# Output chunks of the feed-forward part copied from PSUM by VectorE and ScalarE in turn, with another table of priorities

## The chip, the cores and the metric

The kernel runs on one core of one Trainium2 chip. The core has TensorE (PE in the profile), which multiplies matrices into PSUM, VectorE (DVE), ScalarE (ACT) and GpSimd (POOL) for elementwise work, and SyncE (SP), which here issues most of the DMAs. The metric is device time in microseconds; several executions are timed, and one more is taken by the hardware profiler.

## The reference

Threshold attention over 8 batches and 8 heads (576 positions, head size 64), followed by a gated feed-forward part on the 4608 resulting rows of 512:

```python
scores = scale * np.matmul(q, k.transpose(0, 1, 3, 2))
thresh = np.max(scores, axis=-1, keepdims=True) - tau
scores = np.where(scores >= thresh, scores, -1000000000.0)
attn = np.exp(scores - np.max(scores, axis=-1, keepdims=True))
attn = attn / (np.sum(attn, axis=-1, keepdims=True) + 1e-09)
x = np.matmul(attn, v)                      # heads side by side: 4608 x 512
xn = x / np.sqrt(np.mean(x * x, axis=-1, keepdims=True) + 1e-06) * rms_g
g = xn @ w_gate                             # 512 -> 1536
silu = g * (1.0 / (1.0 + np.exp(-g)))
out = (silu * (xn @ w_val)) @ w_out         # 1536 -> 512
```

## The kernel before

**Work and tiles.** The 4608 rows are cut into 36 chunks of 128 (32 of them 128 positions of one batch, kind "m", and 4 that join the last 64 positions of two batches, kind "v"). For each chunk there are four steps, one for each pair of heads: 144 steps. A step makes the scores of two heads for 128 rows into `s_ps` (PSUM, L697), copies them negated and scaled to `ssb` while it takes their minimum (VectorE, L730), adds tau on GpSimd (L771), and runs one prelu for each head and one exp for both on ScalarE (L782, L789). A DMA transpose on SyncE's queue (L849), in the first 16 steps TensorE (L834), turns the weights into `wt`; two steps together are multiplied with the values (L870, L875), divided by their sum on VectorE (L892, L893) and put into `xsb`. When a chunk's four steps are done, `emit_x` normalises it (square on ScalarE L910, two small operations and a product on GpSimd L913 to L918) and a DMA transposes it into `xnT`.

**The feed-forward part.** `emit_ffn` works on groups of chunks (SIZES: two groups of 2, then eight of 4). For each of 12 blocks of the inner dimension: four matmuls for the gate (L976) and four for the value (L981), each into one PSUM bank of `ring`; tanh on ScalarE (L990), silu on VectorE (L993), product on VectorE (L998) into `hf` (half of its buffers are the staging tile `stg`). Then each chunk of the group gets twelve matmuls with `wo` (L1047) into one bank of `ring`, in two parts of six, and an eviction `ev` copies the bank, multiplied by 0.5, into an output buffer `osb`: a `tensor_scalar` on VectorE (L1062) or an `activation` with Copy on ScalarE (L1064). `store` then writes it out from SyncE's queue (L1075, L1078, L1083). Before the last group two `osb` buffers alternate by chunk. The last group is "streamed" (STREAMED = 1): its four outputs accumulate while its blocks are still computed (L1022), two of its chunks are evicted on VectorE and two on ScalarE, the final one in two halves (L1068 is the first), and ScalarE issues some of its stores.

Which engine evicts a chunk of the other nine groups is chosen by

```python
late = streamed and j % 2
on_dve = streamed and not late or not streamed and OUT_DVE[ci % len(OUT_DVE)]
```

where `ci` is the number of the chunk. `OUT_DVE` is (1,): all 32 go to VectorE.

**What sets the order.** Every operation is added to a list with its engine, an assumed cost, its dependences and a priority in units of steps. `order_ops` then plays the kernel through with the assumed costs: for each engine it takes, of the operations that could start first, the one with the lowest priority number, and the result is written out as the fixed order of each engine's instructions. PSUM banks are handed out in the same pass: `ring` starts with four free banks (two halves of `s_ps` come to it at the end), and an eviction gives its bank back. Before that a table `RANK` shifts priorities, for operations whose priority is 8 or more and not on SyncE; the key is the function that adds the operation and the name of the inner function:

```python
if o.prio >= 8.0 and o.eng != "SP":
    path = o.fn.__qualname__.split(".")
    o.prio += RANK.get(o.eng, {}).get((path[-3] if ... else "main") + "/" + path[-1], 0.0)
```

A positive shift puts an operation behind others that are ready at the same time. The eviction has the priority of its place in the group less 40 (`PUSH[0]`), tanh the same push, silu and the product none. `main/<lambda>` on GpSimd are the four loads of `wo` (L1145), `main/cast` the casts of the other weights (L1133), `emit_block_loads/swap` copies that rearrange k and q (L390), `round_/<lambda>` the casts of v (L584), `emit_softmax/nthr` L771.

Of the kernel before, what the change touches and what calls it, by code (L numbers as in the profile page):

```python
# [12 lines left out]

LAT = dict(PE=200.0, ACT=130.0, DVE=175.0, POOL=20.0, SP=0.0)
SELF = dict(PE=0.0, ACT=125.0, DVE=178.0, POOL=0.0, SP=0.0)
COST = dict(
# [7 lines left out]
SWITCH = 125.0  # L24

RANK = dict(
    ACT={"emit_ffn/ev": 450, "emit_ffn/store": 110, "emit_ffn/tanh": -300, "emit_k_tail/ev": -210, "emit_q_tail/ev": -80, "emit_qk/ev": 370,
        "emit_softmax/ex2": 60, "emit_softmax/prelu": 220, "emit_x/sq": -330},
    DVE={"emit_blocks/turn_k": 120, "emit_blocks/turn_kt": 288, "emit_blocks/turn_q": 293, "emit_burst/ttr": -57.4, "emit_ffn/ev": 320,
        "emit_ffn/gate": 60, "emit_ffn/silu": -59, "emit_k_tail/ev": 80, "emit_qk/ev": -20, "emit_softmax/ev": 320, "emit_x/ev": 50},  # L30
    PE={"emit_av/fn": -370, "emit_burst/fn": 16, "emit_ffn/gmm": 20, "emit_ffn/omm": 23, "emit_ffn/vmm": -40, "emit_k_tail/tr": 210, "emit_q_tail/tr":
        -160, "emit_qk/tr": 60, "emit_softmax/tr": -40, "emit_x/trp": 20},
    POOL={"emit_block_loads/swap": 40, "emit_softmax/nthr": -240, "emit_x/mean": -150, "emit_x/norm": -10, "round_/<lambda>": 130, "main/<lambda>":
        700, "main/cast": -280},
)


# [18 lines left out]
def order_ops(ops, ring_sizes):  # L56
# [26 lines left out]
    while len(out) < len(ops):  # L83
        best = None
        for e, lst in pending.items():
# [5 lines left out]
            for i in lst:  # L91
                o = ops[i]
                t = max(t0, ready_at[i])
                if o.ring is not None:
# [3 lines left out]
                    t = max(t, sorted(free)[o.nring - 1][0])  # L98
                other = e == "PE" and o.mode != mode
                t = max(t, o.release)  # L100
# [11 lines left out]
        cost = o.cost  # L112
        if e == "PE":
            if o.mode != mode:
# [35 lines left out]
def kernel(  # L150
# [98 lines left out]
    def gated(o, step):  # L249
        gates.append((o, step))  # L250
        return o

    def add(eng, cost, prio, deps, fn, **kw):
        o = Op(eng, cost, prio, deps, fn, **kw)
        ops.append(o)
        return o
# [30 lines left out]
    def setup():  # L287
        o_id = add("POOL", 2000.0, -100, [], lambda o: make_identity(nc, id32))

        def zero(o):  # L290
            nc.vector.memset(zcol, 0.0)
            nc.vector.memset(xn[0], 0.0)

        o_z = add("DVE", 350.0, -200, [], zero)

        def warm(o):

            for _ in range(WARM):
                nc.tensor.matmul(s_ps[0][:, 0:512], xn[0][:, 0:128], xn[0], start=True, stop=True)

        o_w = add("PE", WARM * 380.0, -200, [o_z], warm)

        def consts(o):
            nc.vector.tensor_copy(out=id16, in_=id32)
            nc.vector.memset(mhalf, -0.5)

        def vconst(o):
            for i in range(2):
                nc.vector.memset(va[i][:, :, :, D:D + 1], 1.0)
                nc.vector.memset(va[i][64:128, :, 8], 0.0)  # L310
                nc.vector.memset(va[i][0:64, :, 9], 0.0)

        o_c = add("DVE", 300.0, -100, [o_id, o_z], consts)
        o_v = add("DVE", 2000.0, -90, [], vconst)
        o_g = add("SP", 350.0, -0.5, [], lambda o: nc.sync.dma_start(
            out=rmsg, in_=moe_rms_g.rearrange("(c p) -> p c", p=128)), dma=100.0)
        return o_id, o_c, o_v, o_g
# [4 lines left out]
    def emit_qk(b, p, prio):  # L322
# [13 lines left out]
        def tr(o):  # L336
            for j in (1, 0):
                for c in range(4):
                    for r, rs in enumerate(HALF):
# [4 lines left out]

        t = gated(add("PE", COST["tr_qk"], -500.0, los + [o_id] + last_s.get(("k", b - 2, p), []), tr, ring="R",
                      nring=2, mode=1), prio)
        done = []
        for r, rs in enumerate(HALF):
            def ev(o, r=r, rs=rs):
                src = ring[t.slot[r]].rearrange("p (j c n) -> p j c n", j=2, n=64)  # L350
                if EVAC[r] == "ACT":
                    nc.scalar.copy(out=dst[:, :, :, rs], in_=src)
                else:
                    nc.vector.tensor_copy(out=dst[:, :, :, rs], in_=src)

            done.append(add(EVAC[r], COST["evac_qk" if EVAC[r] == "DVE" else "evac_qk_act"], prio, [t], ev, frees=(t, r)))
        for j in range(2):
# [7 lines left out]
    def emit_block_loads(b, g, base, prio):  # L365

        done = {}
        for j, src in ((1, k), (0, q)):
# [14 lines left out]
            for h in range(2):  # L383
# [4 lines left out]
                for dst, at in moves:  # L388
                    def swap(o, dst=dst, at=at):
                        nc.gpsimd.tensor_copy(out=dst, in_=at)  # L390

                    last = [add("POOL", COST["swap"], prio + SWAP_AT, last, swap)]
                spare_use.append(last[0])
# [28 lines left out]
    def emit_first():  # L422
# [13 lines left out]
        def load_k(p, prio):  # L436
# [6 lines left out]

            return add("SP" if p else "ACT", COST["sp_qk"], prio, before, load, dma=DMA_NS["qk"], bulk=True)

# [10 lines left out]
        def transposed(load, srcs, dsts, prio, engines):  # L456
# [9 lines left out]
            for e, (eng, lo, hi) in enumerate(engines):  # L466
                def ev(o, eng=eng, lo=lo, hi=hi):
                    copy = nc.scalar.copy if eng == "ACT" else nc.vector.tensor_copy
                    for i, m, dst in dsts:
                        if lo <= i < hi:  # L470
                            rs = slice(dst.base_partition(), dst.base_partition() + dst.shape[0])
                            copy(out=dst, in_=ring[t.slot[0]][rs, n * i:n * (i + m)].rearrange("p (a n) -> p a n", n=n))
# [13 lines left out]
        def emit_k(p, load, prio):  # L486
            nat = qkn[p % NQK]
            t, k_ready[p] = transposed(load, [pair(nat[:, 1, c]) for c in range(4)],
                                       [(0, 2, qkT[0][p][:, 0, 0:2]), (2, 2, qkT[0][p][:, 0, 2:4])], prio,
                                       [("ACT" if p in (1, 2) else "DVE", 0, 2), ("ACT", 2, 4)])  # L490
            tr_of[1].append(t)
# [84 lines left out]
    def emit_v(b, prio):  # L576
# [6 lines left out]
        def round_(dst, src):  # L583
            return lambda o: nc.gpsimd.tensor_scalar(out=dst, in0=src, scalar1=1.0, scalar2=1.0,  # L584
                                                     op0=ALU.mult, op1=ALU.mult)

        def free(p):
            return [o_v] + last_av.get((b - 2, p), [])

        for p in range(NP):  # L590
# [12 lines left out]
            if b >= BLOCKED and p == 0:  # L603
                lo = []
                for i in range(2 * V_PARTS):
# [8 lines left out]
                    lo[-1].lat = LAT_V  # L614
            ca = add("POOL", COST["cast_v"], (pr + V_CAST if b >= BLOCKED else pr + 1 if b else p - 1.0), (lo[2 * (p * V_PARTS // NP):][:2] if b >= BLOCKED else lo) + free(p), round_(
                t[:, p, 0:8, 0:D].rearrange("q (c h) d -> q h c d", h=2),
# [3 lines left out]
            if p == 0:  # L620
# [6 lines left out]
                for e in range(2):  # L627
                    es = slice(64 * e, 64 * e + 64)
                    ca = add("POOL", COST["cast_vt"], (pr + 1.3 if b else -0.5), [lt] + [x for p in range(NP) for x in free(p)],
                             round_(t[es, :, 8 + e, 0:D], vtl[es]))  # L630
# [322 lines left out]
    def emit_ffn(slot, parts, ready_step, pace, streamed):  # L953
# [81 lines left out]
        for j, (ci, _) in enumerate(parts):  # L1035
# [19 lines left out]
            late = streamed and j % 2  # L1055
            on_dve = streamed and not late or not streamed and OUT_DVE[ci % len(OUT_DVE)]

# [130 lines left out]
TTR_E = 0.0  # L1188
TTR_TO = 16
SQ_DVE = (0,)  # L1190
OUT_DVE = (1,)
LAGS = ()
CHOP = ((32, 144),)
TTR_PRIO = 0.0
# [92 lines left out]
```

## Time and profile before

| | us |
|---|---|
| median of 4 runs | 534.71 |
| lowest and highest of them | 533.09 and 536.46 |
| profiled execution, its own time | 535.12 |
| span of its trace | 533.3 |
| TensorE busy | 521.5 |
| VectorE busy | 465.7 |
| ScalarE busy | 443.9 |
| GpSimd busy | 224.0 |

The trace gives every instruction with its start and duration. In the groups, "out<-in" names the tiles written and read, "x" counts instructions, then come busy microseconds, the mean nanoseconds of one, and the idle time of the engine before them with what ended it. In tables by stage each row is a stretch of the span; the columns are TensorE, its weight load, VectorE, ScalarE and GpSimd with busy microseconds and instruction counts, then the granted clock of TensorE (1.00 is full), the share of the DMA engines in use and GB/s. Ends of matmuls are modelled, so their starts are the safer reading. The first score matmul runs at 6.6 us, the first feed-forward matmul at 62.4, the first output matmul at 89.2, and the first eviction at 93.4.

### The profile page before, as it was taken

What the parts mean: (1) busy time and instruction counts of PE and PEld (TensorE: products, weight loads), DVE (VectorE), ACT (ScalarE), POOL (GpSimd) and SP (SyncE); (2) the same over time, 40 slices, a digit from 0 to 9 for tenths busy, and PEclk for the clock granted to TensorE, in tenths of its full rate; (3) what the DMA queues carried; (4) which work ended last, traced back from release to release, by engine and by line L of the source; (5) the groups of instructions that cost most, each with busy time, mean ns of one, the idle gap of its engine ahead of it and who ended that gap; (6) DMA issues with size and microseconds to landing.
All of it is one profiled execution on the core that took longest, in us unless ns stands there. A gap on an engine that the chain in (4) does not pass through costs nothing.

```text
span 533.3 us, 14401 instructions
## 1 busy us (share of the span) xinstructions
PE 521.5 (98%) x5368; PEld 275.1 (52%) x5368; DVE 465.7 (87%) x1348; ACT 443.9 (83%) x648; POOL 224.0 (42%) x478
## 2 busy tenths in 40 slices
PE   8899999999999999999999999999999999999996
PEld 4566776654545454545454544454544454454442
DVE  4799999979999799989997999999999898865741
ACT  5999999989997899889987898989998999962210
POOL 2278667425762155717733265626652111111000
PEclk9999999999999999999999999999999999999999
DMA  9999989979978888999889798998898678653013
GB/s 186 233 291 299 231 141 190 190 123 242 194 157 170 158 172 182 152 202 207 172 171 176 146 178 172 201 216 166 171 191 139 118 118 134 128 111 70 14 27 98
DMA packets 218886, 88.51 MB, mean 166 GB/s; under 512 B 195264, under 2 KB 204992, under 8 KB 218816
## 3 DMA queue, kind: packets, MB, share of 16 engines
q1 hardware_dynamic: 216016, 85.49, 81.1%
q0 software_dynamic: 1600, 1.57, 1.9%
q8 instruction: 42, 0.69, 0.6%
q10 hardware_dynamic: 1200, 0.52, 0.5%
q14 instruction: 28, 0.23, 0.1%
HBM read 37.75 MB, written 9.44 MB: 88 GB/s over the span
## 4 chain that ended last, share of the span: by engine, by line
PE 63%; DVE 16%; ACT 6%; DMA 5%; issue 4%; POOL 3%; SPq 1%; DVEq 0%; POOLq 0%; ACTq 0%
PE s_ps L697 19%; PE ring L1047 12%; PE ring L981 11%; PE ring L976 11%; DVE ssb L730 10%; PE ring L875 4%; ACT ssb L782 3%; PE s_ps L1022 2%; DVE sl L993 2%; DMA wt<-wsb 2%; DMA qkx<-in_q_dram 2%; DVE hf L998 1%; PE ring L870 1%; ACT wsb L789 1%; PE s_ps L1047 1%
## 5 line engine op out<-in xcount | busy, mean ns | idle before, releaser
L782 ACT ACTIVATE ssb<-ssb,nth 128x576 f32<-128x576 f32 x288 | 209.2, 766 | 21.4 <-POOL nth L771 20.8
L730 DVE CUSTOM_DVE_ANT_0 ssb<-s_ps,zcol 128x576 f32<-128x576 f32 (+8 forms) x288 | 169.4, 635 | 6.5 <-PE s_ps L697 4.9
L697 PE MATMUL s_ps<-qkt 64*64 64x288 f32 (+8 forms) x2256 | 170.4, 412 | 0.8 <-DVE mx L730 0.8
L789 ACT ACTIVATE wsb<-ssb 128x1152 f16<-128x1152 f32 x144 | 166.7, 1158 | 2.6 <-DMA wt<-wsb 0.5
L697 PEld LDWEIGHTS s_ps<-qkt 64*64 64x64 f32 x2256 | 82.1, 134 | 65.4 <-issue 29.0
L976 PE MATMUL ring<-xnT,wg 128*128 128x512 f16 (+1 forms) x464 | 109.2, 358 | 0.6 <-DVE sl L993 0.5
L981 PE MATMUL ring<-xnT,wv 128*128 128x512 f16 (+1 forms) x456 | 107.0, 357 | 0.5 <-DVE sl L993 0.2
L990 ACT ACTIVATE th<-ring 128x512 f32<-128x512 f32 (+1 forms) x116 | 62.5, 541 | 39.4 <-PE ring L976 39.1
L771 POOL TENSOR_SCALAR nth<-mx 128x2 f32<-128x2 f32 x144 | 30.8, 214 | 150.1 <-DVE mx L730 141.2
L993 DVE SCALAR_TENSOR_TENSOR sl<-th,ring 128x512 f32<-128x512 f32 (+1 forms) x116 | 72.0, 623 | 11.3 <-ACT th L990 11.1
L981 PEld LDWEIGHTS <-wv 128*128 128x128 f16 x480 | 44.5, 98 | 50.3 <-issue 11.1
L976 PEld LDWEIGHTS <-wg 128*128 128x128 f16 x480 | 42.9, 98 | 52.6 <-issue 15.1
L730 DVE CUSTOM_DVE_ANT_0 ssb<-s_ps,zcol,mxp 128x128 f32<-128x128 f32 (+7 forms) x112 | 52.9, 509 | 13.7 <-PE s_ps L697 13.6
L875 PE MATMUL ring<-va,wt 128*128 128x65 f16 (+1 forms) x1280 | 51.1, 193 | 0.0
L875 PEld LDWEIGHTS <-wt 128*128 128x128 f16 (+1 forms) x1280 | 46.1, 100 | 5.0 <-issue 0.6
L1047 PE MATMUL ring<-wo,hf 128*128 128x512 f16 x204 | 47.7, 380 | 0.0
L998 DVE TENSOR_TENSOR stg<-ring,sl 128x512 f16<-128x512 f32 (+1 forms) x57 | 35.5, 627 | 2.4
L998 DVE TENSOR_TENSOR hf<-ring,sl 128x512 f16<-128x512 f32 (+1 forms) x57 | 35.5, 626 | 1.8
L1047 PE MATMUL ring<-wo,stg 128*128 128x512 f16 x156 | 36.5, 379 | 0.0
L390 POOL COPY spare<-qkx 32x576 f32<-32x576 f32 x48 | 31.6, 658 | 9.8 <-DMA qkx<-in_k_dram 4.3
L893 DVE TENSOR_TENSOR xsb<-ring,rz 128x256 f32<-128x256 f32 x72 | 30.5, 424 | 3.5
L1047 PEld LDWEIGHTS <-hf 128*128 128x128 f16 x216 | 20.0, 98 | 25.8 <-issue 3.5
(75 smaller groups left out, 483.1 us busy)
## 6 DMA issues: line engine op xcount, KB each, us to landing
vst<-in_v_dram SPq DMA_DIRECT2D x32, 256.0 KB, 4.3
qkx<-in_k_dram SPq DMA_DIRECT2D x24, 288.0 KB, 3.6
qkx<-in_q_dram SPq DMA_DIRECT2D x24, 288.0 KB, 3.8
out_dram<-osb SPq DMA_DIRECT2D x48, 128.0 KB, 2.7
stg<-in_moe_w_gate_dram SPq DMA_DIRECT2D x6, 512.0 KB, 6.1
stg<-in_moe_w_val_dram SPq DMA_DIRECT2D x6, 512.0 KB, 6.1
wt<-wsb SPq DMA_TRANSPOSE x128, 3.6
out_dram<-osb SPq DMA_DIRECT2D x8, 256.0 KB, 3.0
```

Of the source, the lines that this page charges most:

```text
L390: nc.gpsimd.tensor_copy(out=dst, in_=at)
L697: nc.tensor.matmul(s_ps[h][rows, at:at + hi - lo], lhs(hs), k_of(bb, p, h)[hs, lo:hi], start=True, stop=True)
L730: nc.vector.tensor_tensor_reduce(out=ssb_of(s)[:, h, lo:hi], in0=s_ps[h][:, at:at + hi - lo], in1=zcol.to_broadcast([128, hi - lo]), scale ...
L782: nc.scalar.activation(out=sb_[:, h], in_=sb_[:, h], func=PRELU, scale=-1.0, bias=nth[m][:, h:h + 1], **PRELU_KW)
L789: nc.scalar.activation(out=wsb[s % NW], in_=sb_, func=AF.Exp)
L875: nc.tensor.matmul(ring[o.slot[0]][rs, at:at + D + 1], w[:, 5 * h + j, rs], va[vi][:, p, 2 * j + h], start=False, stop=(h == 1 and j == 3))
L976: nc.tensor.matmul(ring[o.slot[0]][:, 0:n], wg[d][:, fs], xnT[slot][:, d, 0:n], start=(d == 0), stop=(d == 3))
L981: nc.tensor.matmul(ring[o.slot[0]][:, 0:n], wv[d][:, fs], xnT[slot][:, d, 0:n], start=(d == 0), stop=(d == 3))
L990: nc.scalar.activation(out=th[i][:, 0:n], in_=ring[g.slot[0]][:, 0:n], func=AF.Tanh, scale=0.5)
L993: nc.vector.scalar_tensor_tensor(out=sl[i][:, 0:n], in0=th[i][:, 0:n], scalar=1.0, in1=ring[g.slot[0]][:, 0:n], op0=ALU.add, op1=ALU.mult)
L998: nc.vector.tensor_tensor(out=hf[hi][:, 0:n], in0=ring[vv.slot[0]][:, 0:n], in1=sl[i][:, 0:n], op=ALU.mult)
L1047: nc.tensor.matmul(ring[(first or o).slot[0]], hf[hs[fc][0]][:, 128 * j:128 * (j + 1)], wo[:, fc], start=(fc == 0), stop=(fc == NFC - 1))
```

## The change

`OUT_DVE` becomes (1, 0): of the 32 chunks before the streamed group those with an even number are evicted by VectorE and those with an odd number by ScalarE. The table `RANK` is another one: some shifts have other values, some are gone (`emit_ffn/ev` on both engines, `emit_x/sq`, `emit_av/fn`, `emit_ffn/vmm`, `main/<lambda>`), and two are new (`emit_av/half`, `emit_ffn/ev_half`). Costs, sizes, buffers and the operations themselves are as they were.

```diff
 RANK = dict(
-    ACT={"emit_ffn/ev": 450, "emit_ffn/store": 110, "emit_ffn/tanh": -300, "emit_k_tail/ev": -210, "emit_q_tail/ev": -80, "emit_qk/ev": 370,
-        "emit_softmax/ex2": 60, "emit_softmax/prelu": 220, "emit_x/sq": -330},
-    DVE={"emit_blocks/turn_k": 120, "emit_blocks/turn_kt": 288, "emit_blocks/turn_q": 293, "emit_burst/ttr": -57.4, "emit_ffn/ev": 320,
-        "emit_ffn/gate": 60, "emit_ffn/silu": -59, "emit_k_tail/ev": 80, "emit_qk/ev": -20, "emit_softmax/ev": 320, "emit_x/ev": 50},
-    PE={"emit_av/fn": -370, "emit_burst/fn": 16, "emit_ffn/gmm": 20, "emit_ffn/omm": 23, "emit_ffn/vmm": -40, "emit_k_tail/tr": 210, "emit_q_tail/tr":
-        -160, "emit_qk/tr": 60, "emit_softmax/tr": -40, "emit_x/trp": 20},
-    POOL={"emit_block_loads/swap": 40, "emit_softmax/nthr": -240, "emit_x/mean": -150, "emit_x/norm": -10, "round_/<lambda>": 130, "main/<lambda>":
-        700, "main/cast": -280},
+    ACT={"emit_ffn/store": 90, "emit_ffn/tanh": -280, "emit_k_tail/ev": -180, "emit_q_tail/ev": -130, "emit_qk/ev": 440, "emit_softmax/ex2": 160,
+        "emit_softmax/prelu": 210},
+    DVE={"emit_av/half": 50, "emit_blocks/turn_k": 140, "emit_blocks/turn_kt": 256, "emit_blocks/turn_q": 260, "emit_burst/ttr": -58,
+        "emit_ffn/ev_half": -40, "emit_ffn/gate": 70, "emit_ffn/silu": -58.6, "emit_k_tail/ev": 70, "emit_qk/ev": -40, "emit_softmax/ev": 250,
+        "emit_x/ev": 60},
+    PE={"emit_burst/fn": 10, "emit_ffn/gmm": 20, "emit_ffn/omm": 23, "emit_k_tail/tr": 240, "emit_q_tail/tr": -300, "emit_qk/tr": 30,
+        "emit_softmax/tr": -2, "emit_x/trp": 10},
+    POOL={"emit_block_loads/swap": 120, "emit_softmax/nthr": -220, "emit_x/mean": -180, "emit_x/norm": 110, "round_/<lambda>": 110, "main/cast":
+        -250},
 )
...
-OUT_DVE = (1,)
+OUT_DVE = (1, 0)
```

## The prediction

> **What bounds the kernel now.** I read the page's head first (span, busy time by engine), then the table by stage, then PE's timeline in a stretch with evictions.
>
> ```profile
> span 533.3 us, 14401 instructions
> ...
> PE 521.5 (98%) x5368; PEld 275.1 (52%) x5368; DVE 465.7 (87%) x1348; ACT 443.9 (83%) x648; POOL 224.0 (42%) x478
> ...
> PE 63%; DVE 16%; ACT 6%; DMA 5%; issue 4%; POOL 3%; SPq 1%; DVEq 0%; POOLq 0%; ACTq 0%
> ```
>
> The third line is the chain that ended last: TensorE carries 63% of it, and the hops through VectorE and ScalarE are short pieces between matmuls. The stages say where the slack lies (TensorE, its weight load, VectorE, ScalarE, GpSimd, each busy us of the stretch):
>
> ```profile
> 20.00:50.00 30.00, 27.48 (x366) 19.33 (x362) 26.89 (x77) 27.47 (x41) 20.34 (x40) 1.00 1.09 285
> 50.00:100.00 50.00, 49.83 (x643) 33.63 (x641) 48.30 (x140) 49.52 (x80) 33.84 (x65) 1.00 0.97 195
> 100.00:150.00 50.00, 50.00 (x568) 26.90 (x565) 46.32 (x149) 46.44 (x69) 25.18 (x54) 1.00 0.96 183
> ...
> 200.00:250.00 50.00, 50.00 (x511) 24.95 (x510) 48.34 (x146) 45.69 (x66) 26.28 (x56) 1.00 1.02 190
> ...
> 400.00:450.00 50.00, 49.49 (x558) 24.24 (x556) 44.61 (x136) 46.26 (x67) 10.18 (x29) 1.00 0.76 127
> ...
> 480.00:500.00 20.00, 20.00 (x109) 9.28 (x106) 13.34 (x21) 5.39 (x10) 1.43 (x3) 1.00 0.21 47
> ```
>
> TensorE is full from 50 us on, at full granted clock, while VectorE and ScalarE run at 87 to 99% beside it until about 475 us; then attention is done and 50 us of feed-forward matmuls remain for which neither is needed much. A busy TensorE need not run at its best pace, so I measured the pace from its timeline:
>
> ```profile
> 215.88 1.04 PE L981 MATMUL ring<-xnT,wv 128*128 128x512 f16 x4
> 216.75 2.75 PE L1047 MATMUL ring<-wo,stg 128*128 128x512 f16 x12
> ...
> 220.03 1.96 PE L697 MATMUL s_ps<-qkt 64*64 64x256 f32 x32
> 221.92 4.06 PE L1047 MATMUL ring<-wo,stg 128*128 128x512 f16 x18
> 225.91 1.96 PE L697 MATMUL s_ps<-qkt 64*64 64x384 f32 x32
> ```
>
> Start to next start: four matmuls 0.87 us, a burst of 32 score matmuls 1.89, eighteen output matmuls 3.99 (0.22 each). I did this for all runs of matmuls of one line, and took from each the shortest time of a run with the same count and shapes and the same kind of successor (score burst or not). What is above that is TensorE's lost time: 14.7 us in all, of it 2.6 in 0 to 20, 3.3 in 20 to 50, 2.6 in 50 to 100, then by stretches of 50 us 0.82, 1.17, 0.48, 0.89, 0.63, 0.96, 1.06 (sum 6.0 from 100 to 450), and 0.2 after that. The matmuls themselves are not touched by the change, so a gain must come out of these 14.7 us, and the first evicted output chunk starts only at 93.4 us: for the evictions themselves at most about 6 us are there to be won.
>
> **The evictions (OUT_DVE).** Nine of the ten feed-forward groups, 32 chunks, are evicted on VectorE now; the last, streamed group keeps its own rule. With (1, 0) the 16 chunks with an odd index go to ScalarE. The prices:
>
> ```profile
> L1062 DVE TENSOR_SCALAR osb<-ring 128x512 f32<-128x512 f32 x30 | 20.1, 676 | 10.5 <-PE ring L1047 10.5
> ...
> L1064 ACT ACTIVATE ssb<-s_ps 128x512 f32<-128x512 f32 x1 | 0.6, 597 | 8.9 <-PE s_ps L1022 8.9
> ```
>
> and, from VectorE's timeline, two in a row:
>
> ```profile
> 225.39 1.28 DVE L1062 TENSOR_SCALAR osb<-ring 128x512 f32<-128x512 f32 x2
> ```
>
> VectorE gives back 16 x 0.676 = 10.8 us (two in a row took 1.28, so at least 16 x 0.60 = 9.6, the second start being one 0.68 before the end); ScalarE takes 16 x 0.597 = 9.6 us (less where the next follows at once: in ScalarE's timeline the 0.57 us tanh at 177.66 had its successor start at 178.13, so at least 16 x 0.47 = 7.5). Busy time becomes about 455 on VectorE and 453 on ScalarE. Stores stay on SyncE, in the same number and with the same buffer for each chunk, since chunk parity was already buffer parity.
>
> VectorE's relief: in the seven stretches from 100 to 450 us TensorE's loss does not follow VectorE's load (48.3 busy with 0.48 lost, 44.6 with 1.06), so I take 0; at best half of the 6.0 us goes, -3, and it can cost nothing.
>
> ScalarE's load: the 9.6 us spread over about 375 us, 1.3 more in each 50. Behind a waiting eviction on ScalarE stand prelu and exp of the next softmax steps (2 x 0.77 + 1.16 us a step), and behind these SyncE's transpose of the weights, the attention-value matmuls and the score buffers. Two rows bound it. Against 100 to 450 (mean 45.56 busy, 0.86 lost) the stretch 50 to 100 (49.52 busy, 2.63 lost) gives 1.77/3.96 = 0.45 us lost for one of load: +4.3. Within the seven stretches the loss does not rise with ScalarE's load (43.3 busy with 0.89, 46.4 with 0.63 to 0.96): 0. I take +1.5, nearer to the seven, which are the stage concerned.
>
> The function change on ScalarE costs nothing by the trace. The page has one table load for the whole kernel, though ScalarE changes between prelu, exp, tanh, square and copies all along:
>
> ```profile
> L472 ACT ACT_TABLE_LOAD x1 | 1.3, 1283 | 1.5 <-PEq L1268 1.5
> ```
>
> If each of the 16 copies brought two such loads, ScalarE would get 16 x 2 x 1.283 = 41 us more; the two copies at 526 and 528 us brought none, so I take 0. ("ScalarE: Activation LUTs", Table sets, asks to batch calls by set and puts a switch at some 2.7 us, which would speak against the change; 32 switches would be 86 us by it. It also says that cheap functions like copy are in every set, and that agrees with the row.) "TensorEngine Tiling (Array Packing)", PSUM Bottleneck, says to use both engines for evacuation, which by itself would make this a gain of up to VectorE's 10.8 us; the trace shows TensorE full without it, so the sum has 0 for that.
>
> **The priorities (RANK).** They reorder every engine but SyncE's own entries, for operations with a due step of 8 or more. Evictions on VectorE go from rank +320, behind everything ready, to 0 with their push of 40: ahead of all but reductions, silu and input copies. In the trace evictions started 0.04 to 5.88 us after their last matmul (216.75 + 2.75 = 219.51 against 225.39 above). A sooner eviction frees one of four banks sooner; TensorE lost 0.48 us in that very stretch, so this is worth 0 to -0.5, and I take 0. On VectorE the attention output drops to +50; on TensorE attention-value goes from -370 to 0 and the value matmul from -40 to 0; on ScalarE the square goes from -330 to 0. Work only changes places, TensorE's queue runs strictly as written, and every place in which the written order is wrong by a few tenths of a us is lost. The largest single losses after 100 us were 0.64, 0.48 and 0.35. Bounds: half of the 8.5 us lost before 100 us is recovered (-4), or one 0.3 us wait comes with each of the 16 moved chunks and the early stage loses as much again as it does from 20 to 100 (+4.8 + 5.9 = +10.7). No row of the trace favours a side, and I take 0.
>
> The loads of the output weights on GpSimd lose their +700. They go out at 41.9 to 59.7 us now, with the DMA engines at share 1.0; earlier they push 1.5 MB ahead of other loads, each 384 KB / 285 GB/s = 1.4 us. All four lie inside the full stage already, so the total there does not change: 0, bounds -1.4 and +1.4. The swaps, at rank 120 instead of 40, come later on GpSimd, which is busy 42% of the time: 0.
>
> The tail is the same: streamed group, last evictions and stores are unchanged (520 to 533 us).
>
> **Sum.** +1.5 us on the profiled execution's 535.12 us (span 533.3 and 1.8 around it) is 536.6; that execution lies 0.4 above the median of the runs, 534.71, so the forecast for the median is 536.2.
>
> **The rivals.** About 0.5%, 2.7 us, is what a measurement of this kernel can tell from no change.
>
> Slower by more than that: ScalarE becomes late. It is at 93% in the full stages and goes to about 95%; in a row of three prelus and an exp a copy in the middle, waiting for its twelfth matmul, holds back softmax, and TensorE finds neither scores nor gates ready. For: 50 to 100 us, the one stretch with ScalarE at 99%, loses three times as much as the others. Against: 475 to 525 us holds 50 us of matmuls that can be drawn forward when attention is late. It decides from 0.17 us lost for each moved chunk on (2.7/16); at 0.3 it gives 534.7 + 4.8 = 539.5, with the early stage worse too up to 545.
>
> Faster: VectorE is what ends the small waits, and with 10.8 us less on it and banks freed at once half of the 6.0 us goes, with a part of the early loss: 534.7 - 3 - 1 = 530.7. For: VectorE is the busier of the two, and it carries 16% of the chain. Against: the losses do not follow its load.
>
> That it does nothing on the chip but swap slack is the forecast itself, with TensorE full: 533 to 537.
>
> **How the numbers follow.** Forecast case (within 0.5%) 0.43, ScalarE late 0.38, VectorE's relief 0.19. The forecast's own range is 532 to 537.4; to leave out no more than 2 in 10 it reaches to 530.7 below and 542.5 above. Slower has more than faster, since 6 us can be won in the stage concerned and more can be lost.
>
> **What would show it.** VectorE near 455 and ScalarE near 453 us busy; 16 copies from line 1064 near 0.6 us on osb; still one table load; TensorE's matmul count unchanged and its lost time, counted as above, near 16 us. Score bursts or gate matmuls that wait for prelu or tanh say ScalarE is late. The prediction is wrong if the new order loses time in the first 100 us, or if it wins there what I give to no one.

## The result, and the profile after

The changed kernel takes 535.1 us (median of 51 runs, 533.79 to 538.34) against 534.28 for the kernel before beside it (74 runs); the ratio is 1.0016, 95% interval 1.0010 to 1.0022. That is 0.85 us slower, by the bound of 0.5% no change. The prediction was 536.2, in a range of 530.7 to 542.5, with "within 0.5%" as the likeliest case. The profiled execution took 534.77 us (span 533.0), 0.35 less than the one before the change, so 0.85 us cannot be looked for in the two traces.

The head of the page after: span, busy time by engine, and the chain that ended last.

```profile
span 533.0 us, 14390 instructions
...
PE 521.4 (98%) x5368; PEld 276.1 (52%) x5368; DVE 455.7 (86%) x1332; ACT 451.0 (85%) x664; POOL 224.2 (42%) x478
...
PE 85%; DVE 6%; DMA 3%; issue 2%; POOL 1%; SPq 1%; ACT 1%; DVEq 0%; POOLq 0%
```

VectorE went from 465.7 to 455.7, ScalarE from 443.9 to 451.0, TensorE stayed. The chain now has 85% TensorE instead of 63%, which looks like a great change and is worth nothing: its shares moved without any time moving. (Perhaps because, where three engines are nearly full, a chain followed back through one may as well be followed through another; no run shows it.) The groups of the evictions and the table load:

```profile
L1063 DVE TENSOR_SCALAR osb<-ring 128x512 f32<-128x512 f32 x15 | 10.2, 679 | 4.5 <-PE ring L1048 3.7 <-DMA out_dram<-osb 0.8
...
L1065 ACT ACTIVATE osb<-ring 128x512 f32<-128x512 f32 x16 | 9.4, 585 | 17.2 <-PE ring L1048 12.3 <-DMA out_dram<-osb 4.9
...
L473 ACT ACT_TABLE_LOAD x1 | 1.3, 1283 | 1.5 <-PEq L1269 1.5
```

(Lines after the table are one higher than before.) Sixteen copies on ScalarE at 585 ns, and still one table load. By stage (TensorE, its weight load, VectorE, ScalarE, GpSimd busy us, then clock, DMA share, GB/s):

```profile
50.00:100.00 50.00, 50.00 (x644) 33.58 (x637) 48.22 (x140) 48.95 (x79) 33.45 (x65) 1.00 0.92 193
100.00:150.00 50.00, 50.00 (x566) 27.52 (x569) 45.03 (x147) 47.11 (x71) 24.65 (x54) 1.00 0.93 181
...
200.00:250.00 50.00, 50.00 (x509) 25.32 (x507) 47.08 (x147) 45.45 (x67) 25.84 (x54) 1.00 0.96 185
...
400.00:450.00 50.00, 50.00 (x575) 24.94 (x574) 44.56 (x137) 48.25 (x69) 9.92 (x30) 1.00 0.81 130
```

TensorE's lost time, counted by the prediction's rule, is 14.7 us: 2.4 in 0 to 20, 3.5 in 20 to 50, 2.9 in 50 to 100, then 1.11, 1.03, 1.09, 0.93, 0.74, 0.31 and 0.47 by stretches of 50 us (5.7 from 100 to 450). For the kernel before, the prediction's 14.7 is 0.7 too small. Between two steps of attention-value matmuls at 290.3 us, 0.68 us are lost while TensorE waits for the transposed attention weights (the last bracket is the idle time and what ended it):

```profile
291.25 0.23 PE L870 MATMUL ring<-va,wt 128*128 128x130 f16 x1 [0.50 <-DMA wt<-wsb]
```

With it the kernel before loses 15.4 us, 6.7 of them from 100 to 450 us and 1.57 instead of 0.89 in 250 to 300; it is also the largest single loss after 100 us. The readings of the prediction stand with these numbers.

This count is the yardstick of all that follows. As an estimate, time moves by what is added to or taken from TensorE's work plus the change of its lost time:

| run | lost time, us | ratio to the kernel before, 95% interval |
|---|---|---|
| before | 15.4 | 1 |
| changed kernel | 14.7 | 1.0016 (1.0010 to 1.0022) |
| engines alone | 15.2 | 1.0000 (0.9990 to 1.0010) |
| table alone | 16.6 | 1.0007 (0.9993 to 1.0022) |
| evictions twice, VectorE | 24.0 | 1.0166 (1.0151 to 1.0181) |
| evictions twice, ScalarE | 16.6 | 1.0043 (1.0029 to 1.0058) |
| fewer matmuls | 20.8 | 0.9863 (0.9839 to 0.9887) |
| half copies | 15.8 | 1.0009 (0.9993 to 1.0024) |
| more on VectorE, elsewhere | 31.0 | 1.0298 (1.0266 to 1.0330) |
| more on ScalarE | 24.3 | 1.0188 (1.0164 to 1.0212) |
| all on ScalarE | 19.8 | 1.0085 (1.0055 to 1.0114) |
| tiny copies | 14.5 | 1.0025 (1.0005 to 1.0045) |
| fewer matmuls, tiny copies | 19.0 | 0.9829 (0.9800 to 0.9857) |
| all but one on ScalarE | 15.0 | 1.0011 (0.9998 to 1.0024) |

(In the run with all on ScalarE the score burst ahead of its longest wait is written as 16 matmuls of 128 rows instead of 32 of 64, as the kernel does where another burst follows at once. It is the only one of its shapes in that trace, so there is nothing to compare it with; to the counted 17.0 I added the wait behind it, 2.84 us, as the profile gives it. The profiled executions of two runs, evictions twice on VectorE and all on ScalarE, were granted a clock of 0.67 and 0.66 from 25 to 30 us, where all others had 1.00; from 20 to 50 us they lost 4.6 and 5.6 us, the kernel before 3.3. So some 1 to 2 us of these two lost times are the clock's, by estimate.)

### The profile page after: what moved, and what is told of

The parts are those of the page before. It is cut to its first block, busy times and chain, and to the rows that moved or that the text cites. A ratio compares the mean times of both kernels' runs of the same rounds, so it can differ in the third digit from the quotient of the medians.

```text
span 533.0 us, 14390 instructions
## 1 busy us (share of the span) xinstructions
PE 521.4 (98%) x5368; PEld 276.1 (52%) x5368; DVE 455.7 (86%) x1332; ACT 451.0 (85%) x664; POOL 224.2 (42%) x478
## 3 DMA queue, kind: packets, MB, share of 16 engines
q0 software_dynamic: 1600, 1.57, 1.8%
## 4 chain that ended last, share of the span: by engine, by line
PE 85%; DVE 6%; DMA 3%; issue 2%; POOL 1%; SPq 1%; ACT 1%; DVEq 0%; POOLq 0%
PE s_ps L698 27%; PE ring L982 16%; PE ring L1048 15%; PE ring L977 14%; PE ring L876 6%; DVE ssb L731 4%; PE s_ps L1023 2%; PE ring L871 2%; PE s_ps L977 2%; DMA qkx<-in_q_dram 1%; DMA qkx<-in_k_dram 1%; DVE sl L994 1%; PE ring L835 1%; DMA stg<-in_q_dram 1%; PE s_ps L1048 0%
## 5 line engine op out<-in xcount | busy, mean ns | idle before, releaser
L731 DVE CUSTOM_DVE_ANT_0 ssb<-s_ps,zcol 128x576 f32<-128x576 f32 (+8 forms) x288 | 169.3, 634 | 6.2 <-PE s_ps L698 5.2
L982 PE MATMUL ring<-xnT,wv 128*128 128x512 f16 (+1 forms) x476 | 112.0, 358 | 0.4
L977 PE MATMUL ring<-xnT,wg 128*128 128x512 f16 (+1 forms) x440 | 103.1, 357 | 0.5 <-DVE sl L994 0.5
L994 DVE SCALAR_TENSOR_TENSOR sl<-th,ring 128x512 f32<-128x512 f32 (+1 forms) x110 | 68.2, 620 | 10.9 <-ACT th L991 10.9
L991 ACT ACTIVATE th<-ring 128x512 f32<-128x512 f32 (+1 forms) x110 | 59.2, 538 | 14.8 <-PE ring L977 14.1
L731 DVE CUSTOM_DVE_ANT_0 ssb<-s_ps,zcol,mxp 128x128 f32<-128x128 f32 (+7 forms) x112 | 52.9, 509 | 19.4 <-PE s_ps L698 19.0
L999 DVE TENSOR_TENSOR stg<-ring,sl 128x512 f16<-128x512 f32 (+1 forms) x60 | 37.6, 630 | 2.7
L1048 PE MATMUL ring<-wo,stg 128*128 128x512 f16 x168 | 39.1, 379 | 0.0
L999 DVE TENSOR_TENSOR hf<-ring,sl 128x512 f16<-128x512 f32 (+1 forms) x59 | 36.8, 629 | 1.7
L914 POOL TENSOR_SCALAR irm<-ssq 128x1 f32<-128x1 f32 x36 | 6.9, 191 | 64.6 <-ACT xn L911 63.9
```

The source lines that it names most:

```text
L731: nc.vector.tensor_tensor_reduce(out=ssb_of(s)[:, h, lo:hi], in0=s_ps[h][:, at:at + hi - lo], in1=zcol.to_broadcast([128, hi - lo]), scale ...
L977: nc.tensor.matmul(ring[o.slot[0]][:, 0:n], wg[d][:, fs], xnT[slot][:, d, 0:n], start=(d == 0), stop=(d == 3))
L982: nc.tensor.matmul(ring[o.slot[0]][:, 0:n], wv[d][:, fs], xnT[slot][:, d, 0:n], start=(d == 0), stop=(d == 3))
L991: nc.scalar.activation(out=th[i][:, 0:n], in_=ring[g.slot[0]][:, 0:n], func=AF.Tanh, scale=0.5)
L994: nc.vector.scalar_tensor_tensor(out=sl[i][:, 0:n], in0=th[i][:, 0:n], scalar=1.0, in1=ring[g.slot[0]][:, 0:n], op0=ALU.add, op1=ALU.mult)
L999: nc.vector.tensor_tensor(out=hf[hi][:, 0:n], in0=ring[vv.slot[0]][:, 0:n], in1=sl[i][:, 0:n], op=ALU.mult)
```

## The experiments

My theory was that TensorE is full and the evictions lie beside it, so that moving them is worth nothing either way. The rivals: ScalarE becomes late; VectorE is what paces the kernel and its relief was eaten up elsewhere; the two parts of the change, engines and table, have effects that cancel.

**The two parts alone.** Engines alone, with the old table:

```diff
-OUT_DVE = (1,)
+OUT_DVE = (1, 0)
```

> Only the engines of the 16 odd chunks change, with the old table of priorities (whose entry +450 puts evictions on ScalarE behind all else that is ready). TensorE is full: ratio to the kernel before 0.995 to 1.005, most likely 1.000 to 1.003, VectorE some 10 us less busy and ScalarE some 7 to 9 us more. ScalarE is late: 1.005 to 1.01. Two effects that cancel (the engines gain, the table loses): 0.993 to 0.997.

Measured: 1.0000 (0.9990 to 1.0010); VectorE 456.4 and ScalarE 450.4 us busy. Table alone, the new `RANK` with `OUT_DVE = (1,)`:

> Only the table of priorities changes; all 32 chunks are still evicted by VectorE, now early in its order. TensorE is full: 0.997 to 1.005. Two effects that cancel (the engines gain, the table loses): 1.004 to 1.010, so that this run is slower than the whole change. Busy times of all engines as before within 2 us.

Measured: 1.0007 (0.9993 to 1.0022). Neither part has an effect of 0.3%, so nothing of that size cancels. The 0.16% of the whole cannot be put on one of them: the table's interval holds it, and the engines' interval ends below it, at 0.10%.

**More load at a fixed order.** The kernel's planner writes the order from assumed costs. If an operation emits more than its assumed cost covers, the order stays and only the load grows. First each eviction on VectorE twice, in the kernel before:

```diff
+                    for _ in range(1 if streamed else 2):
-                    nc.vector.tensor_scalar(out=osb[oi][:, cols], in0=ring[mo.slot[at]][:, cols], scalar1=0.5, ...)
+                        nc.vector.tensor_scalar(out=osb[oi][:, cols], in0=ring[mo.slot[at]][:, cols], scalar1=0.5, ...)
```

> The kernel before, its order untouched, with each of the 32 evictions on VectorE done twice: 32 x 0.60 to 0.68 = 19 to 22 us more on VectorE, 10 us more than the change takes off it. TensorE is full and an eviction lies beside it: 0 to +4 us (1.000 to 1.008). VectorE sets the pace wherever it is over 93% busy: +10 to +20 us (1.019 to 1.037).

Measured: 1.0166 (1.0151 to 1.0181), 8.9 us. VectorE was 486.7 us busy, 21.0 more, so 0.42 us lost for one of load. Neither expectation holds: the load is not hidden, and it does not pass in full.

```profile
100.00:150.00 50.00, 49.28 (x552) 27.00 (x545) 47.40 (x149) 45.64 (x66) 24.44 (x53) 1.00 0.91 175
150.00:200.00 50.00, 48.85 (x533) 24.64 (x531) 47.86 (x140) 43.57 (x63) 19.05 (x41) 1.00 0.89 170
...
250.00:300.00 50.00, 48.72 (x482) 23.98 (x480) 48.29 (x141) 42.99 (x62) 26.32 (x54) 1.00 0.91 166
```

These are stages of that run: VectorE 47.4 to 48.3 of 50, and TensorE for the first time under 49. The same on ScalarE, in the changed kernel (its 16 copies, twice):

> The changed kernel, its order untouched, with each of the 16 evictions on ScalarE done twice: 16 x 0.48 to 0.58 = 7.7 to 9.3 us more on ScalarE, as much again as the change put there. TensorE is full: within 2 us of the changed kernel (ratio to the kernel before 1.000 to 1.005). ScalarE is late, at 0.3 us lost for each moved chunk: 4.8 us on top (1.008 to 1.012). At 0.45 us for one of load, the steeper of the two slopes of the prediction: 3.5 to 4.2 us on top.

Measured: 1.0043 (1.0029 to 1.0058), 0.27% or 1.4 us above the changed kernel, for 8.6 us more busy time on ScalarE (459.6): 0.17 for one. The first and mildest of the expectations, the one of a TensorE that is full.

A doubled eviction also holds its PSUM bank for longer. So the next run let the bank go after one copy and put the load elsewhere, in place on the output buffer:

```diff
+                    for _ in range(0 if streamed else 2):
+                        nc.vector.tensor_scalar(out=osb[oi][:, cols], in0=osb[oi][:, cols], scalar1=1.0, ...)
```

> The kernel before, its order untouched; each of the 32 chunks is evicted once, its bank is free after that, and then VectorE multiplies the output buffer by one twice, in place (32 x 2 x 0.3 to 0.68 = 19 to 44 us more on VectorE). What cost 8.9 us with doubled evictions is VectorE's load: at least 0.35 us lost for each us of load added (7 to 20 us, 1.013 to 1.037). It is the bank, which came free one copy later: under 0.15 us for one of load (1.000 to 1.008).

Measured: 1.0298 (1.0266 to 1.0330), 15.9 us for 29.2 us more on VectorE (494.9): 0.54 for one. It is VectorE's load, not the bank (the second of the two expectations, under 0.15 for one, is out). And as much load on ScalarE as the doubled evictions had put on VectorE, in the changed kernel:

```diff
-            def ev(..., cols=slice(DM // 2 if final else 0, DM)):
+            def ev(..., cols=slice(DM // 2 if final else 0, DM), n=1 if streamed else 3 + (ci % 4 == 1)):
...
-                    nc.scalar.activation(out=osb[oi][:, cols], in_=ring[mo.slot[at]][:, cols], func=AF.Copy, scale=0.5)
+                    for _ in range(n):
+                        nc.scalar.activation(out=osb[oi][:, cols], in_=ring[mo.slot[at]][:, cols], func=AF.Copy, scale=0.5)
```

> The changed kernel, its order untouched, with the 16 evictions on ScalarE done three or four times, 40 extra copies: 40 x 0.54 = 21.5 us more on ScalarE (8.6 us for 16 by the profile of the doubled ones), as much as the doubled evictions put on VectorE (21.0). ScalarE has more slack than VectorE: +2 to +5.5 us on the changed kernel (ratio to the kernel before 1.005 to 1.012). ScalarE is as near to its limit as VectorE: +8 to +11 us (1.016 to 1.022).

Measured: 1.0188 (1.0164 to 1.0212), 9.2 us above the changed kernel for 21.6 us more on ScalarE (472.6): 0.43 for one. This is the second expectation: as much load costs on ScalarE what it costs on VectorE (0.42 at 21.0). In 100 to 200 us its stages show it at 48.3 and 46.9 and TensorE at 48.8 and 48.5 of 50:

```profile
100.00:150.00 50.00, 48.82 (x544) 26.86 (x545) 44.03 (x142) 48.26 (x73) 23.64 (x52) 1.00 0.89 177
150.00:200.00 50.00, 48.48 (x526) 24.29 (x522) 44.09 (x132) 46.88 (x69) 18.49 (x41) 1.00 0.81 166
```

Here no run separates the longer hold of the bank from the load, as for VectorE; but in this trace no instruction is seen to wait for the copies.

The traces show where the load comes out. A score burst can start only when VectorE has read the burst before it out of `s_ps` (L730, L731 after the change). From 100 to 450 us no matmul of the kernel before, or of the changed one, stood idle for that; only weight loads did, beside running matmuls (16 times each in 100 to 475 us, 6.8 and 6.3 us in all). With the load added matmuls wait too: evictions twice on VectorE, more on VectorE elsewhere, and more on ScalarE (us in all, times, longest):

```profile
PE s_ps L697 <- DVE mxp L730: 2.7, 5, 0.7
PE s_ps L697 <- DVE mxp L730: 5.9, 9, 1.4
PE s_ps L698 <- DVE mxp L731: 3.6, 7, 1.1
```

So part of ScalarE's load, too, comes out at VectorE's reductions, and VectorE itself was held up by ScalarE: its waits for tanh, in the changed kernel and then with more on ScalarE, and for exp, in the latter alone:

```profile
DVE sl L994 <- ACT th L991: 2.8, 3, 1.7
DVE sl L994 <- ACT th L991: 9.6, 10, 3.6
DVE ssb L731 <- ACT wsb L790: 2.8, 6, 1.0
```

The matmuls' waits for the reductions are about a third of the time lost on top (2.7 of 8.6, 5.9 of 15.6, 3.6 of 9.6 us). The rest is in other waits and in runs of matmuls that are slower without a wait that the profile names.

**Less load at a fixed order.** Adding load costs; does taking load away gain? The evictions of the kernel before, cut to half their columns (a memset at the start, 0.5 us on VectorE, sets the other half to zero):

```diff
-            def ev(..., cols=slice(DM // 2 if final else 0, DM)):
+            def ev(..., cols=slice(DM // 2 if final else 0, DM if streamed else DM // 2)):
```

> The kernel before, its order untouched, with the 32 evictions on VectorE cut to half their columns (the other half of each output row is left out and stays at zero): 32 x (0.68 - 0.425) = 8.2 us less on VectorE, about what the change takes off it, at a fixed order and with nothing added to ScalarE. TensorE is full and VectorE's relief is worth nothing: 0.997 to 1.001. The slope of the doubled evictions (8.9 us for 20, 0.43 each) holds downward too: -3.5 us (0.993). Then the change gained 4 us by VectorE and lost it elsewhere.

Measured: 1.0009 (0.9993 to 1.0024), with VectorE at 458.4. No gain: 0.4 us at most by the interval. The changed kernel with all 32 evictions cut to 16 columns by the same edit (VectorE 449.8, ScalarE 445.5 us busy):

> The changed kernel, its order untouched, with the 32 evictions cut to 16 columns (the rest of each output row is left out and stays at zero): about 8 us less on VectorE and 6 less on ScalarE, so next to nothing is left of the evictions on either. TensorE is full: ratio to the kernel before 0.998 to 1.002, and no placing of the evictions can gain anything. If the slope of the added loads (0.43 us for one) holds downward: -3 to -6 us (0.989 to 0.995).

Measured: 1.0025 (1.0005 to 1.0045). Even evictions that cost next to nothing gain nothing: against the changed kernel's 1.0016 that leaves at most some 0.6 us (an estimate from the two intervals), in this order of instructions, for any placing of the evictions. So VectorE's evictions do not pace the kernel. Its other work, the score reductions above all, was not taken away in any run. The curve is flat below where the kernel stands and rises above it, more steeply the further it goes: on ScalarE 0.17 us for one over the first 8.6 and, from there to 21.6, 7.8 us for 13.0, 0.60 for one. Where it begins to rise is not measured on VectorE, whose first point is 21.0 us up.

**Less work for TensorE.** Two of each twelve output matmuls left out in the kernel before, its order fixed:

```diff
-                        for fc in range(lo, lo + OUT_PART):
+                        for fc in [f for f in range(lo, lo + OUT_PART) if f % 6 != 1]:
```

> The kernel before, its order untouched, with two of the twelve output matmuls (blocks 1 and 7) of each of the 32 chunks left out, so the output lacks those two blocks: 64 x 0.216 = 13.8 us less on TensorE, nothing less on the other engines. TensorE is full: 11 to 13.8 us faster (ratio 0.974 to 0.980). VectorE, 93 to 97% busy in the full stages and dear when its evictions were doubled (+8.9 us), is a bound beside it: 3 to 9 us faster (0.983 to 0.994).

Measured: 0.9863 (0.9839 to 0.9887), 7.3 us of the 13.8. The lost time rose by 5.4 us, from 6.7 to 11.8 of it in 100 to 450: the second expectation. TensorE is the bound, but only by some microseconds; with less to do it waits (for VectorE's score reductions 1.9 us from 100 to 450, before none). With tiny copies on VectorE as well:

> The kernel before, its order untouched, with both two of twelve output matmuls of the 32 chunks left out (-13.8 us on TensorE; alone that gave -7.3 us) and the evictions on VectorE cut to 16 columns (about -16 us on VectorE; at half width, -7.3 us busy, it gave nothing). The output lacks these parts. Balanced engines, where VectorE is the next limit once TensorE has less to do: -9.5 to -13 us (0.976 to 0.982). If VectorE's evictions are off every path and what holds the rest of the 13.8 us is the order or ScalarE: -7 to -8.5 us (0.984 to 0.987).

Measured: 0.9829 (0.9800 to 0.9857), 9.1 us, between the two expectations. VectorE's evictions, worth nothing alone, seem to be worth 1.8 us once TensorE is lighter. The intervals of the two runs overlap; the lost times (20.8 and 19.0) and TensorE's wait for the reductions (1.9 and 0.6 us) point the same way. What holds back the other 4.7 us, ScalarE or the fixed order, stays open.

**More evictions on ScalarE, with the order planned for it.** `OUT_DVE = (0,)` in the changed kernel:

> The changed kernel with all 32 chunks evicted by ScalarE and the order planned for that: another 8 us or so on ScalarE (about 459 busy) and 10 less on VectorE (about 445). By the doubled copies on ScalarE (+8.6 us, +1.4 us) a little slower than the changed kernel: ratio to the kernel before 1.002 to 1.006. If the planner, which knows of the load, finds an order that hides it: 0.999 to 1.002. If ScalarE alone now sets the pace, at the 0.43 us for one of load of the tripled copies: 1.006 to 1.010.

Measured: 1.0085 (1.0055 to 1.0114), 3.7 us above the changed kernel, with ScalarE at 458.1. By the ratio that is the third expectation. But the lost time is not spread: from 150 to 450 us it is 3.2 us, less than the 5.9 of the kernel before. Of what is lost on top, 2.3 us lie in 20 to 50 us, before any eviction, where the granted clock of the profiled execution fell to 0.66 (the number ahead of the last two):

```profile
25.00:30.00 5.00, 5.00 (x62) 3.96 (x60) 2.56 (x6) 2.90 (x5) 1.60 (x4) 0.66 1.07 276
```

Part of the 4.5 us over the kernel before is therefore the clock: the five executions run from 536.49 us at a mean granted clock of 1.000 to 540.37 at 0.992, and the first of these is 2.0 above the kernel before's median. What the placing of the evictions lost sits in one place:

```profile
121.01 2.00 PE L698 MATMUL s_ps<-qkt 64*128 64x256 f32 x16
125.86 2.23 PE L698 MATMUL s_ps<-qkt 64*64 64x384 f32 x32 [2.84 <-DVE mxp L731]
128.02 0.23 PE L871 MATMUL ring<-va,wt 128*128 128x130 f16 x1
...
128.63 1.02 PE L977 MATMUL ring<-xnT,wg 128*128 128x512 f16 x4
129.49 1.03 PE L982 MATMUL ring<-xnT,wv 128*128 128x512 f16 x4
131.49 2.08 PE L698 MATMUL s_ps<-qkt 64*64 64x512 f32 x16 [0.97 <-DVE mxp L731]
```

Two score bursts follow each other, and the second waits until VectorE has read the first out of `s_ps`, the wait that the added loads brought out too. There is nothing else in between, because the gate matmuls of the next group of four chunks come only at 128.63: their last chunk was transposed late, by SyncE's timeline of that run,

```profile
125.39 1.21 SPq L923 DMA_TRANSPOSE xnT<-xn  x1
```

against 118.92 in the kernel before. So the last run gave VectorE one of the 32 chunks back, the first, and left 31 on ScalarE:

```diff
-OUT_DVE = (0,)
+OUT_DVE = (1,) * 1 + (0,) * 35
```

> As with all evictions on ScalarE, but the first of the 32 chunks goes to VectorE again; the other 31 stay on ScalarE, whose busy time stays at about 458. The 4.3 us of that run were lost in one place, a written order with two score bursts in a row near 122 us because the feed-forward matmuls had run out, which this order does not have: ratio to the kernel before 0.998 to 1.004, lost time of TensorE in 100 to 150 us about 1. ScalarE's load as such cost the 4.3 us: 1.006 to 1.010 as before.

Measured: 1.0011 (0.9998 to 1.0024), with ScalarE at 457.8 us, as busy as in the run before; from 100 to 150 us it lost 1.5 us, where the run before lost 5.6 with the added wait. Its timeline at that place (the transpose is at 117.99):

```profile
120.43 1.96 PE L698 MATMUL s_ps<-qkt 64*64 64x384 f32 x32
122.33 1.04 PE L977 MATMUL ring<-xnT,wg 128*128 128x512 f16 x4
123.20 1.03 PE L982 MATMUL ring<-xnT,wv 128*128 128x512 f16 x4
124.06 1.03 PE L977 MATMUL ring<-xnT,wg 128*128 128x512 f16 x4
124.93 1.03 PE L982 MATMUL ring<-xnT,wv 128*128 128x512 f16 x4
125.88 1.95 PE L698 MATMUL s_ps<-qkt 64*64 64x512 f32 x16
```

The burst is followed by the four groups of feed-forward matmuls that were missing. The cost of the run with all on ScalarE was, beside the clock, the order at one place, not ScalarE's load: 14 us more on ScalarE than in the kernel before, with 17.6 less on VectorE (448.1), cost nothing that can be measured. The doubled copies had brought ScalarE to 459.6 us, about as far, at 1.0043 without being in the plan; VectorE was 8 us busier there. Which of the two made the difference, the plan or VectorE's lighter load, is not shown. Why the engine of the first eviction moves the fourth chunk's transpose by 7 us was not followed further.

No run was faster than the kernel before with all of its work done; none of the places tried for the evictions beats it.

## Why the prediction was right

**TensorE full, its matmuls untouched.** Right for this change: the matmuls are the same 5368, the lost time 15.4 before and 14.7 after. As a general statement it was too strong: only 7.3 of 13.8 us of matmuls taken away came through, so VectorE, ScalarE or the order are some microseconds behind TensorE, and not far behind as "full" suggests.

**VectorE's relief, taken as 0 (bounds -3 and 0).** Right, and shown twice at a fixed order: half copies 1.0009, tiny copies 1.0025. VectorE's 455 us came as forecast (455.7). The prediction read it from the fact that the loss does not follow VectorE's load from stretch to stretch. That reading holds downward only; upward the same engine costs 0.42 to 0.54 us for one of load.

**ScalarE's load, taken as +1.5 (bounds 0 and +4.3).** The term that was too large. The engines alone measured 0.0 (-0.5 to +0.5 us), and 31 chunks on ScalarE +0.6 us (-0.1 to +1.3). ScalarE's own rise was smaller too, 7.1 us (451.0) instead of 9.6, which is 0.44 for a copy and below the prediction's own lower bound of 7.5. The lower row, "the seven stretches", was the right one for this change, whose load the planner knows and which takes 10 us off VectorE. A slope like the upper row's 0.45 for one appeared only with load that the order was not made for and that VectorE did not give up: 0.43 on ScalarE in the run with 40 extra copies. That the two agree so closely is luck: from 50 to 100 us, where the upper row comes from, the work is another mix, with no eviction before 93.4 us (feed-forward matmuls are in it from 47.7 us on; the 62.4 given ahead of the prediction is a later one).

**No table load for copies, taken as 0.** Right: one load of 1283 ns in the changed kernel, as the row before had it.

**The priorities, taken as 0 (bounds -4 and +10.7).** The table alone gave +0.4 us (-0.4 to +1.2). Right in size, and the bounds were far too wide. The sooner eviction that the prediction described is there in the middle but not in the extreme: the median delay from the modelled end of a chunk's last matmul to its eviction fell from 0.71 to 0.36 us, while the longest stayed (5.88 us at 225.4, now 5.82 at 225.9, on ScalarE). Neither moved time, as the prediction had it.

**The loads of the output weights, taken as 0 (bounds -1.4 and +1.4).** They went out at 41.6 to 55.5 us instead of 41.9 to 59.7, and landed in 8.1 us instead of 7.3. The lost time from 20 to 100 us is 6.4 instead of 5.9, in one execution each.

**The tail.** As predicted: the lost time after 450 us is 0.2 before and 0.3 after.

**The sum and the rivals.** +1.5 was forecast on the median, +0.85 measured; the remaining 0.4 us of the 1.1 between 536.2 and 535.1 is the kernel before itself, 534.71 in four runs and 534.28 in 74. The size came close in part by luck: +1.5 was a choice between 0 and +4.3, the term that it stands for measured 0.0, and the runs of the parts do not say where the 0.85 lies. The mechanism, slack swapped beside a full TensorE, is what happened. Of the rivals, ScalarE late has a real slope, but not for this change: it took load added at a fixed order, or an order that runs out of feed-forward matmuls, to bring a loss out. VectorE's relief as a gain is refuted for its evictions.

## What to carry to other kernels

An engine at 95% beside a full one says nothing yet about what a microsecond on it is worth: measure both signs, by doubling the operation and by cutting it down at a fixed order; here the one gave half a microsecond and the other nothing. Where the order is written ahead, ask of a moved operation whether the planner knows its cost and whether some queue runs dry at a place, and look at the lost time and the granted clock stretch by stretch before blaming an engine's load. The lost time of the busiest engine, counted from start to next start against the best of its kind, followed the times above 1% off (both ways) to within some 1.1 us and the small ones to within 2.2 us, so it says nothing of differences of a microsecond. The chain of waits did worse: its share of TensorE rose from 63 to 85% where the time moved by 0.16%.

## What the runs showed of the hardware

In the run with the load elsewhere VectorE's multiply of 128x512 float32 took 677 ns from PSUM and 480 ns on average, 428 in the median, from SBUF in place. In the run with tiny copies a copy of 128x16 out of PSUM took 173 ns on ScalarE and 163 on VectorE, 30 and 24% of the 585 and 679 ns of a copy 32 times as wide in the changed kernel. At a granted clock of 0.66 a score burst of eight matmuls took 2.08 us from its start to the next start (25.86 us in the run with all on ScalarE), at 1.00 the same burst took 1.08 (24.08 us in the run with all but one there).
